# The fold of a unit in two steps, with another unit's masks in between, and one pair of logits behind a key copy

## The chip, the cores and the metric

The kernel runs on one core of one Trainium2 chip. The metric is the device time of one execution in microseconds (us). Engines are named as the profile names them: PE (matrix multiply; PEld is its weight load), DVE (vector), ACT (scalar), POOL (GpSimd) and SP, which here only issues DMAs. A name with a q behind it is the engine's sequencer or queue.

## The reference

Two blocks, one after the other, for 4 batches, 8 heads, 768 tokens and 48 channels per head (384 channels in all), in float32.

```python
f = 1.0 / (1.0 + np.exp(-f_logit))                       # attention with a gate
for t in range(S):
    state = f[:, :, t, :, None] * state + np.einsum('bhd,bhe->bhde', k[:, :, t], v[:, :, t])
    y[:, :, t] = np.einsum('bhd,bhde->bhe', q[:, :, t], state)

X = np.fft.fft(np.fft.fft(x, axis=1), axis=2)            # x: y as (B, S, H*D)
u = x + np.real(X)
un = (u - mean(u)) / np.sqrt(var(u) + 1e-06)
out = u + np.maximum(un @ w_ch1, 0.0) @ w_ch2            # 384 -> 1536 -> 384
```

## The kernel before

**Units.** Two heads of one batch make a unit: 16 units, unit u belongs to batch u // 4. Each unit is a Python generator, `attention(u)`, that goes on in `outputs(u)`; each `yield` ends a step. The steps, with their lines before the change: (1) the logits, two activations on ACT (L330, L331); (2) a running sum on DVE (L337, L338; L339 on POOL); (3) exponentials on ACT (L342, L343, L345); (4) two products on DVE (L349, L350); (5) 48 score matmuls (L361) into two PSUM tiles `sc`; (6) the masks: two copies under a mask on DVE, one per `sc` tile (L368); (7) the keys transposed on PE (L506, tile `st`) and copied by ACT to `kT` (L508); (8) `ds` on PE (L517); (9) a scan of the states on DVE (L525); (10) and (11) `y` on PE (L537, L544) and its copies on ACT (L553 to L557, tile `yT`); (12) transposes back (L564) and a copy to `x` (L566); (13) the fold.

`sc`, `st`, `ds` and `yt` share two PSUM buffers in turn, so the transposes of step 7 have to wait for the first mask of step 6, and `ds` for the second.

**The fold** adds and subtracts the halves of a batch's tokens, so that the Fourier transform over tokens needs less work. Its first part (L590 to L596) makes `eo` from `x`; L590 and L594 to L596 are on POOL, or on DVE in the last unit of a batch, and L591 to L593 on DVE. In the first two units of a batch it ends there. In the third and fourth a second part follows on DVE: `xs` (L604) and `xc` (L608), which read `eo` also in what POOL wrote, and in the fourth also `se` (L606), a second `xs` (L607), and `ce` and `xc` (L610 to L612).

**The Fourier part**, `fnet(b)`, begins with four terms `z` on PE (L650): from `se`, `xs`, `ce` and `xc` in this order, each against the table `tab`. ACT copies each term to `zz` (L653 to L657). The terms, and much else, use a PSUM pool of two buffers (`ps_f`): the third term needs what the copies of the first release. Then come `mid` (L684) and `mix` (L669) on PE, the sum with `x` and the moments on DVE (L686, L687, L725, L691, L692, L728, L730), a normalised row `un` (L705), its transposes `pt` (L708), and the two layers `up` (L750) and `fx`, `fz`, `po` (L773, L759).

**Tables and weights.** `tables()` (word T) issues the loads of `tab` and, from POOL, one indirect DMA (L183). `sort_tables()` (word S) puts them in order on POOL: L197 and L198 on `tab`, then L201 to L209 on `cd` and `half`, which `mid` and `mix` read. The weights come as 64-bit words; `weights()` (word C) turns a block into float32 with ACT (L238), DVE (L240, L241) and POOL (L242).

**What sets the order.** The order is written out by hand: `ORDER` is a string of words, and each word makes one piece of the program issue its instructions. A number runs the next step of that unit; `D` issues four matmuls without use (L153) that keep PE busy; `L7fk` issues the DMAs of unit 7's f and k; `F0`, `H0` and `P0` run steps of batch 0's Fourier part and layers; `r` fetches weights. Every engine executes its own instructions in the order in which the words issued them, and waits for the others by semaphores alone.

Of the kernel before, what the change touches and what calls it, by code (L numbers as in the profile page):

```python
# [12 lines left out]
C = 128  # L13
# [14 lines left out]
    "Gq2 r I D Gq0 L0f Gk1 L1f D Gk0 L0q i D Gq3 C Gq1 Z L0k 0 D 1 Gk2 0 L1q 1 L1k D D D D D D D D D D D "  # L28
    "D 0 0 1 0 r 1 L2f 0 2 C L1v 1 L3fk 1 3 L0v 0 1 L2q 2 0 0 r 1 L2k 3 1 0 2 r 3 L3q 2 L2v 0 C L3v C "
    "L4fk R 4 2 2 3 1 0 C 2 4 1 3 L5qv D L4qv L5fk 3 D D 3 2 0 2 3 2 3 C r 4 1 4 L6fk C r 2 5 4 L6qv 4 2 "  # L30
    "1 5 6 3 4 D 4 C 5 3 T 3 6 4 5 5 4 2 r L7fk 7 5 D L7qv 3 5 S L8fk C 4 7 6 6 5 F0 5 r r F0 F0 F0 7 4 "
    "C F0 L9fk 5 6 8 H0 H0 6 5 6 r H0 C L8qv 6 7 L9qv P0 6 7 r C P0 7 7 C 9 P0 r r 5 8 C r C F0 r 7 F0 6 "
    "P0 5 9 C 6 7 P0 r C P0 8 8 C P0 r r 7 P0 P0 8 9 H0 C P0 P0 8 7 8 C P0 H0 7 9 6 H0 H0 C 9 r C P0 9 "
    "L10fk r 9 P0 r C 9 L11fk 10 C 6 P0 11 4 P0 P0 P0 P0 P0 P0 10 P0 P0 P0 L10qv P0 P0 7 F1 9 P0 F1 H0 9 "
    "W P0 P0 P0 11 F1 P0 L11qv P0 P0 P0 9 P0 P0 P0 8 L12fk P0 11 11 8 P0 P0 10 11 F1 P0 11 11 10 L14fk "
    "F1 8 P0 14 F1 P0 10 P0 8 10 P0 P0 H1 H1 10 L12qv P0 P0 10 P0 F1 P0 11 11 10 P0 10 H1 P0 P0 P0 P0 12 "
    "12 12 P0 P0 12 P0 H1 P0 12 P0 H1 L13fk P1 P1 P1 P1 P1 14 13 P1 12 8 8 P1 P1 12 9 10 L13qv 13 P1 P1 "
    "L14qv 9 P1 12 11 P1 H1 11 10 P1 P1 13 P1 13 P1 12 P1 P1 14 P1 14 V 13 P1 c V 10 P1 P1 P1 P1 P1 V "
    "L15fk P1 13 P1 11 V P1 P1 P1 P1 c P1 11 F2 V c F2 F2 H1 13 H1 F2 c 14 P1 c V c P1 P1 12 P1 P1 14 P1 "
    "P1 13 V V V P1 15 F2 c P1 12 P1 P1 P1 P1 c P1 H2 14 15 V V P1 P1 P1 P1 P1 13 P1 14 F2 P1 c P1 P1 15 "  # L40
    "V 13 P1 H2 P1 P1 L15qv P1 14 13 P1 V 12 H2 F2 14 P2 P2 P2 P2 P2 P2 P2 15 P2 P2 P2 c c 12 H2 V H2 15 "
    "H2 15 P2 c P2 15 P2 P2 15 P2 14 13 15 P2 P2 14 P2 P2 15 13 P2 P2 P2 P2 P2 H2 V 15 P2 P2 14 15 H2 P2 "
    "P2 P2 P2 15 F3 F3 P2 F3 F3 P2 F3 c P2 P2 P2 P2 P2 V P2 c P2 V c c V P2 P2 P2 P2 P2 c P2 F3 F3 P2 V "
    "P2 H3 P2 P2 P2 H3 H3 P2 P2 P2 P2 P2 P2 P2 P2 P2 P2 P3 H3 c P3 P3 P3 P3 V P3 c P3 P3 P3 c V V c P3 "
    "P3 P3 H3 P3 P3 P3 P3 P3 P3 c P3 P3 V P3 H3 P3 P3 P3 P3 P3 P3 H3 H3 P3 P3 P3 P3 P3 P3 P3 P3 P3 P3 P3 "
    "P3 V P3 P3 P3 P3 P3 c P3 c P3 P3 P3 M P3 P3 P3 P3 P3 P3 P3 P3 P3 P3 P3 P3"
)

PAIRS = ((0, 3), (2, 5), (1, 4))
# [4 lines left out]
def kernel(  # L54
# [14 lines left out]
    B, HP, _, D, _, S = qkf.shape  # L69
# [426 lines left out]
    def outputs(u, x_all, AT, Q, K, te, T=None):  # L496

        hp = u % HP
        vt = v_of.pop(u)
        ps = ps_a.tile([128, 2, 512], F32, tag="sc", name=f"st{u}").rearrange("p a b -> p (a b)")
        for c in range(NCH - 1):
            nc.tensor.transpose(ps[:, c * 128:c * 128 + R], K[:, c * C:(c + 1) * C], ident[:R, :R])  # L506
        kT = p2.tile([128, NCH - 1, R], F32, tag="kT", name=f"kT{u}")
        nc.scalar.copy(kT, ps[:, :(NCH - 1) * 128].rearrange("p (c k) -> p c k", k=128)[:, :, :R])  # L508
        yield

        ps = ps_a.tile([128, 2, 512], F32, tag="sc", name=f"ds{u}")
        ds = ps[:, 0, :NCH * D].rearrange("p (e c) -> p e c", c=NCH)
        for c in range(NCH - 1):
            for r in range(2):

                n = 1 if c < NCH - 2 else 2
                nc.tensor.matmul(ds[FILL[r], :, c:c + n], lhsT=kT[:, c, FILL[r]],  # L517
                                 rhs=vt[:, c, r * D:(r + 1) * D].unsqueeze(2).to_broadcast([128, D, n]),
                                 start=True, stop=True)
        yield  # L520

        st = p2.tile([128, D, NCH], F32, tag="st", name=f"stt{u}")
        if te is not None:
            flat = lambda a: a.rearrange("p e c -> p (e c)")
            nc.vector.tensor_tensor_scan(flat(st[:R]), ps[:R, 0, :NCH * D], flat(te), 0.0, ALU.add, ALU.mult)  # L525
        else:
            nc.vector.tensor_copy(st[:R, :, 0], ds[:R, :, 0])
            for c in range(1, NCH - 1):
                nc.vector.scalar_tensor_tensor(st[:R, :, c], st[:R, :, c - 1], T[:, c:c + 1], ds[:R, :, c],
                                               ALU.mult, ALU.add)  # L530
        yield

        y = y_out

        for c in range(NCH):
            for r in range(2):
                nc.tensor.matmul(y[FILL[r], c * C:(c + 1) * C],  # L537
                                 lhsT=vt[:, c, r * D:r * D + (64 if r == 0 else D)], rhs=AT[:, r, c],
                                 start=(c % 4 == 0), stop=(c == 0), skip_group_check=True)
        yield  # L540

        for c in range(1, NCH):
            for r in range(2):
                nc.tensor.matmul(y[ROWS[r], c * C:(c + 1) * C], lhsT=st[ROWS[r], :, c - 1],  # L544
                                 rhs=Q[ROWS[r], c * C:(c + 1) * C], start=False, stop=True,
                                 skip_group_check=True)


        yT = p2.tile([128, S], F32, tag="yT", name=f"yT{u}")[:R]
        to = yT.rearrange("p (a n) -> p a n", n=C)  # L550
        rest = yT[:, 4 * C:].rearrange("p (a n) -> p a n", n=C // 2)
        of = y[:R, :S].rearrange("p (a n) -> p a n", a=4)
        nc.scalar.copy(to[:, 0:4:3, 1:], of[:, 0::2, 1:C])  # L553
        nc.scalar.copy(to[:, 1:3, 1:], of[:, 1::2, QS - 1:QS - C:-1])
        nc.scalar.copy(rest[:, 0::3], of[:, 0::2, C:])
        nc.scalar.copy(rest[:, 1:3], of[:, 1::2, QS - C:0:-1])
        nc.scalar.copy(to[:, 0:4, 0], of[:, :, 0])  # L557
        if te is None:
            load(u + 4, "q", "v")
        yield  # L560

        ps = ps_a.tile([128, 2, 512], F32, tag="sc", name=f"yt{u}").rearrange("p a b -> p (a b)")
        for c, i in enumerate((0, 1, 4, 2, 3, 5)):
            nc.tensor.transpose(ps[:, c * 128:c * 128 + R], to[:, i], ident[:R, :R])  # L564
        x = x_all()
        nc.scalar.copy(  # L566
            x[:, :, hp * 2 * D:(hp + 1) * 2 * D].rearrange("t c (r e) -> t c r e", r=2),
            ps[:, :NCH * 128].rearrange("t (c r k) -> t c r k", r=2, k=64)[:, :, :, :D])
        yield
        fold(u, x)  # L570

    eo_of = {}

    def fold(u, x):

        b, hp = divmod(u, HP)
        if b not in eo_of:
            eo_of[b] = p1.tile([128, 8, DM], F32, tag="eo", name=f"eo{b}")
        eo = eo_of[b] if hp < HP - 1 else eo_of.pop(b)
        ch = slice(hp * 2 * D, (hp + 1) * 2 * D)
        f = eo[:, :, ch]
        last = hp == HP - 1
        other = nc.vector if last else nc.gpsimd
        other.tensor_tensor(f[:, 6:3:-1], x[:, 0:3, ch], x[:, 3:6, ch], ALU.subtract)  # L590
        nc.vector.tensor_tensor(f[:, 1:4], x[:, 0:3, ch], x[:, 3:6, ch], ALU.add)  # L591
        nc.vector.tensor_tensor(f[:, 0:8:7], f[:, 1:7:5], f[:, 2:6:3], ALU.add)
        nc.vector.tensor_tensor(f[:, 2:6:3], f[:, 1:7:5], f[:, 2:6:3], ALU.subtract)  # L593
        other.tensor_copy(f[:, 1:7:5], f[:, 0:8:7])  # L594
        other.tensor_copy(f[0:1, 0], f[0:1, 2])
        other.tensor_tensor(f[0:1, 2:7:4], x[0:1, 0:2, ch], x[0:1, 3:5, ch], ALU.subtract)  # L596
        if hp < HP // 2:
            return


        lo, hi = (QD + 1, HD) if hp == HP // 2 else (1, QD + 1)
        up = slice(DM - lo, DM - hi, -1)
        tt = nc.vector.tensor_tensor
        tt(xs[:, :, lo:hi], eo[:, 4:7, lo:hi], eo[:, 4:7, up], ALU.subtract)  # L604
        if last:
            tt(se[:, :, 1:QD], xs[:, :, 1:QD], xs[:, :, HD - 1:QD:-1], ALU.subtract)  # L606
            tt(xs[:, :, 1:QD + 1], xs[:, :, 1:QD + 1], xs[:, :, HD - 1:QD - 1:-1], ALU.add)  # L607
        tt(xc[:, :, lo:hi], eo[:, 0:4, lo:hi], eo[:, 0:4, up], ALU.add)  # L608
        if last:
            nc.vector.tensor_copy(xc[:, :, 0:HD + 1:HD], eo[:, 0:4, 0:HD + 1:HD])  # L610
            tt(ce, xc[:, :, 0:QD + 1], xc[:, :, HD:QD - 1:-1], ALU.add)
            tt(xc[:, :, 0:QD], xc[:, :, 0:QD], xc[:, :, HD:QD:-1], ALU.subtract)  # L612
# [270 lines left out]
    with tc.If(again > 0):  # L883
# [13 lines left out]
        for b in range(B):  # L897
            x = p2.tile([128, NCH, DM], F32, tag="x", name=f"again{b}")
# [76 lines left out]
```

## Time and profile before

| | |
|---|---|
| median of 4 runs | 553.88 us (553.18 to 555.04) |
| the profiled execution | 554.22 us, its span 552.4 us, mean PE clock 0.983 |
| busy share of the span | PE 95%, PEld 84%, DVE 54%, ACT 35%, POOL 17% |
| chain that ended last | PE 88%, DVE 3%, DMA 2%, POOL 2%, ACT 2% |
| largest lines of the chain | PE up L750 34%, fx L773 16%, fz L773 12%, z L650 4% |

The span is what the profiler saw on the core; the device time has 1.8 us more around it. A line of the timeline gives the start and the length in us, the engine, the source line, the operation, the tile that is written and the tiles that are read, and in brackets how long the engine stood idle before it and who ended that. The releaser in the bracket is inferred: it is the last of the candidates to have ended. A line of the windows gives the length and then for PE, PEld, DVE, ACT and POOL the busy time with the number of instructions, and at the end the PE clock that was granted (1.00 is full), the share of DMA time, and GB/s.

### The profile page before, as it was taken

The page shows a single profiled execution, that of the slowest core. Times are in us where ns is not written, and L with a number is a line of the kernel's source. Part 1 is how long each engine was busy: PE and PEld are TensorE (multiplying, and loading weights), DVE is VectorE, ACT ScalarE, POOL GpSimd, SP SyncE. Part 2 cuts the span into 40 slices and gives each one's busy share as a digit, 9 for nine tenths or more (in the row PEclk, how much of TensorE's full clock was granted, in tenths as well). Part 3 has the DMA queues.
Part 4 walks back from the last instruction along what each step waited for, and adds up shares of the span by engine and source line. Part 5 has one row for each costly group of instructions (what it writes and reads, how often), then busy time and mean ns, then how long its engine had stood idle before and what let it go on. Part 6 is the DMA issues. An engine that isn't in the chain of part 4 may idle for free.

```text
span 552.4 us, 10204 instructions
## 1 busy us (share of the span) xinstructions
PE 526.7 (95%) x4186; PEld 462.0 (84%) x4186; DVE 300.0 (54%) x534; ACT 192.4 (35%) x497; POOL 94.9 (17%) x147
## 2 busy tenths in 40 slices
PE   6787699999999999999999999999999999999995
PEld 5676578876898889889889899899889798989985
DVE  8999899984936427436644344444452441413231
ACT  6767466671332432441340422321411303021110
POOL 6155635534001000120101001003001000010000
PEclk9798889999999999999999999999999999999999
DMA  8989636363202100412530401002002004000001
GB/s 229 272 222 230 180 115 162 123 187 95 67 0 72 42 3 2 116 44 65 178 115 15 115 1 59 28 1 87 1 28 87 1 13 159 0 30 0 30 2 34
DMA packets 18398, 44.38 MB, mean 80 GB/s; under 512 B 3109, under 2 KB 4710, under 8 KB 18342
## 3 DMA queue, kind: packets, MB, share of 16 engines
q1 hardware_dynamic: 17094, 39.89, 25.7%
q0 software_dynamic: 1104, 3.54, 1.8%
q8 instruction: 35, 0.57, 0.4%
q10 hardware_dynamic: 144, 0.20, 0.1%
q14 instruction: 21, 0.17, 0.1%
HBM read 38.90 MB, written 4.72 MB: 79 GB/s over the span
## 4 chain that ended last, share of the span: by engine, by line
PE 88%; DVE 3%; DMA 2%; POOL 2%; ACT 2%; issue 1%; ACTq 0%; POOLq 0%; DVEq 0%
PE up L750 34%; PE fx L773 16%; PE fz L773 12%; PE z L650 4%; PE y L537 3%; PE sc L361 3%; PE y L544 3%; PE po L759 3%; PE mix L669 3%; PE ds L517 2%; PE yt L564 2%; DMA tab<-in_seq_tab_dram,back 1%; PE pt L708 1%; PE st L506 1%; DVE at L368 1%
## 5 line engine op out<-in xcount | busy, mean ns | idle before, releaser
L750 PE MATMUL up<-unT,w 128*128 128x256 f32 x864 | 197.0, 382 | 1.5 <-DVE x L728 0.9
L750 PEld LDWEIGHTS up<-unT,w 128*128 128x128 f32 x864 | 160.9, 190 | 26.1 <-issue 1.5
L752 ACT ACTIVATE h<-up 128x256 f32<-128x256 f32 x144 | 55.1, 382 | 199.6 <-PE up L750 199.6
L617 POOL DMA_INDIRECT out_dram<-x,place x16 | 16.9, 1056 | 270.4 <-DVE x L803 233.7
L773 PE MATMUL fx<-block,h 128*128 128x192 f32 x264 | 46.5, 326 | 0.0
L773 PE MATMUL fx<-w,h 128*128 128x192 f32 x264 | 44.9, 327 | 0.1
L773 PEld LDWEIGHTS fx<-w,h 128*128 128x128 f32 x264 | 43.1, 190 | 0.8 <-ACT h L752 0.4
L773 PEld LDWEIGHTS fx<-block,h 128*128 128x128 f32 x264 | 43.5, 190 | 0.0
L780 DVE TENSOR_TENSOR s<-h,h 128x768 f32<-128x768 f32 x11 | 10.5, 955 | 50.4 <-ACT h L752 50.4
L242 POOL TENSOR_TENSOR w<-w,raw 128x384 uint32<-128x384 uint32 x24 | 29.9, 1250 | 46.3 <-ACT raw L238 18.9
L361 PE MATMUL sc<-q,W 48*64 48x128 f32 x768 | 26.1, 281 | 6.5 <-issue 3.6
L368 DVE COPY_PREDICATED at<-causal,sc 128x768 f32<-128x768 uint32 x32 | 31.3, 1031 | 1.1 <-PE sc L361 1.1
L361 PEld LDWEIGHTS sc<-q,W 48*64 48x64 f32 x768 | 21.6, 136 | 10.2 <-issue 5.9
L337 DVE TENSOR_TENSOR_SCAN W<-g,bound 112x768 f32<-112x768 f32 x16 | 29.5, 1844 | 0.5 <-issue 0.4
L725 DVE TENSOR_TENSOR x<-mix,x 128x384 f32<-128x384 f32 x12 | 6.7, 556 | 38.9 <-PE mix L669 38.9
L537 PE MATMUL y<-at,v 128*64 128x128 f32 (+1 forms) x384 | 26.7, 291 | 0.0
L537 PEld LDWEIGHTS y<-at,v 128*64 128x64 f32 (+1 forms) x384 | 23.0, 139 | 3.2 <-issue 3.2
L773 PE MATMUL fz<-w,s 128*128 128x192 f32 x132 | 23.5, 328 | 0.0
L773 PE MATMUL fz<-block,h 128*128 128x192 f32 x132 | 23.5, 328 | 0.0
L773 PE MATMUL fz<-w,h 128*128 128x192 f32 x132 | 23.4, 327 | 0.0
L773 PEld LDWEIGHTS fz<-w,s 128*128 128x128 f32 x132 | 21.6, 190 | 0.3 <-issue 0.3
L773 PEld LDWEIGHTS fz<-block,h 128*128 128x128 f32 x132 | 21.6, 190 | 0.3
(145 smaller groups left out, 730.4 us busy)
## 6 DMA issues: line engine op xcount, KB each, us to landing
raw<-in_w_ch_dram SPq DMA_DIRECT2D x24, 384.0 KB, 4.5
g<-in_qkf_dram SPq DMA_DIRECT2D x32, 144.0 KB, 4.0
q<-in_qkf_dram SPq DMA_DIRECT2D x32, 144.0 KB, 4.0
k<-in_qkf_dram SPq DMA_DIRECT2D x32, 144.0 KB, 5.1
v<-in_v_dram SPq DMA_DIRECT2D x16, 288.0 KB, 4.9
k<-in_w_ch_dram SPq DMA_DIRECT2D x12, 384.0 KB, 3.8
g<-in_w_ch_dram SPq DMA_DIRECT2D x12, 384.0 KB, 4.2
out_dram<-x SPq DMA_DIRECT2D x4, 168.0 KB, 2.1
```

The costliest lines, as they stand in the source:

```text
L242: nc.gpsimd.tensor_tensor(bits, bits, lo, ALU.add)
L337: nc.vector.tensor_tensor_scan(W, g, bound[:R], 0.0, ALU.add, ALU.min)
L361: nc.tensor.matmul(ps[64 * s:64 * s + 64, r, i * C:(i + 1) * C], lhsT=W[ROWS[r], o + 64 * s:o + 64 * s + 64], rhs=Q[ROWS[r], o:o + C], sta ...
L368: nc.vector.copy_predicated(AT[:, :, half], causal.bitcast(U32).unsqueeze(1).unsqueeze(1).to_broadcast([128, 2, NCH // 2, C]), ps[:, :, :N ...
L537: nc.tensor.matmul(y[FILL[r], c * C:(c + 1) * C], lhsT=vt[:, c, r * D:r * D + (64 if r == 0 else D)], rhs=AT[:, r, c], start=(c % 4 == 0), ...
L544: nc.tensor.matmul(y[ROWS[r], c * C:(c + 1) * C], lhsT=st[ROWS[r], :, c - 1], rhs=Q[ROWS[r], c * C:(c + 1) * C], start=False, stop=True, s ...
L617: nc.gpsimd.indirect_dma_start(out=out.rearrange("b s d -> (b s) d"), out_offset=bass.IndirectOffsetOnAxis(ap=place[:, b, i:i + 1], axis=0 ...
L650: nc.tensor.matmul(z[:, cols], lhsT=src[:, j, lo:hi], rhs=tab[:, t, T % 2, cols], start=(i == 0), stop=(i == len(parts) - 1), skip_group_c ...
L669: nc.tensor.matmul(mix[:, o], lhsT=zz[:rows_of[T], T, PLACES[c]], rhs=cd[:rows_of[T], T, :NQ - odd], start=(i == 0), stop=(i == 1))
L750: nc.tensor.matmul(pp[:, :256], lhsT=w1[:, kt, m * 128:(m + 1) * 128], rhs=unT[:, kt], start=(kt == 0), stop=(kt == 2))
L752: nc.scalar.activation(hs[-1][:, m % H].rearrange("p t n -> p (t n)"), pp[:, :256], AF.Relu)
L773: nc.tensor.matmul(out, lhsT=h[:, m], rhs=blocks[i][:, m], start=(start and m == 0), stop=(m == H - 1), skip_group_check=True)
```

## The change

`fold` becomes a generator that yields between its two parts, so the second part needs a word of its own in `ORDER`. Units 2, 3, 6, 7, 10, 11, 14 and 15 (those with a second part) have 14 words instead of 13. In seven of them the new word stands directly behind the old one. In unit 2 the masks of unit 5 (its sixth step) stand between. And unit 7's first step, which stood ahead of those masks, goes behind the seventh step of unit 5, the transposes and the copy of its keys.

```diff
         yield
-        fold(u, x)
+        yield from fold(u, x)
...
         if hp < HP // 2:
             return
+        yield
...
-    ... 5 5 4 2 r L7fk 7 5 D L7qv 3 5 S L8fk C 4 7 6 6 5 F0 ...
+    ... 5 5 4 2 r L7fk 5 2 D L7qv 3 3 5 7 S L8fk C 4 7 6 6 5 F0 ...
-    ... 10 C 6 P0 11 4 ...
+    ... 10 C 6 6 P0 11 4 ...
```

The last pair stands for the places of units 7, 10, 11, 14 and 15 too, where a second number stands behind the first in the same way. Behind `ORDER` the source lines move down by one, and behind the new `yield` by two: L330 becomes L331, and L604 becomes L606.

In the order of each engine this leaves two differences. DVE: from L593 (unit 2), L604 and L608 (unit 2), two L368 (unit 5), L590 (unit 3) to L593, two L368, L604 and L608, L590. ACT: from L566 (unit 3), L330 and L331 (unit 7), L508 (unit 5), L238 to L566, L508, L330 and L331, L238. The order on PE, POOL and SP is the same as before.

## The prediction

> **What bounds the kernel now.** I read the page first, then the windows, then the chain that ended last, and then the timeline of each engine around the edit. TensorE is busy for 95% of the span, so a change counts only where it lets TensorE start sooner. The windows say where that can be:
>
> ```profile
> 65.00:70.00 5.00, 2.77 (x23) 1.89 (x18) 4.72 (x12) 3.36 (x11) 3.80 (x10) 0.89 0.32 93
> 100.00:552.00 452.00, 444.00 (x3087) 394.11 (x3085) 207.66 (x393) 127.75 (x353) 47.90 (x67) 1.00 0.18 53
> ```
>
> The columns are PE, PEld, DVE, ACT, POOL busy, then the clock. After 100 us PE is packed at full clock, so a shift in its start there lasts to the end. Between 65 and 70 us PE works 2.77 of 5 us while DVE works 4.72: this stage is DVE's. The edit lies just ahead of it. On PE and DVE:
>
> ```profile
> 64.63 0.85 PE L517 MATMUL ds<-v,kT 128*64 128x48 f32 x20
> 67.70 1.70 PE L650 MATMUL z<-tab,se 128*95 128x385 f32 x6 [2.23 <-POOL half L207]
> 69.19 2.77 PE L650 MATMUL z<-tab,xs 128*96 128x385 f32 x6
> ...
> 58.98 0.36 DVE L593 TENSOR_TENSOR eo<-eo 128x192 f32<-128x192 f32 x1
> 60.83 0.46 DVE L604 TENSOR_TENSOR xs<-eo 128x285 f32<-128x285 f32 x1 [1.49 <-POOL eo L596]
> 61.66 1.96 DVE L368 COPY_PREDICATED at<-causal,sc 128x768 f32<-128x768 uint32 x2
> 63.52 0.43 DVE L590 TENSOR_TENSOR eo<-x 128x288 f32<-128x288 f32 x1
> 67.15 0.46 DVE L606 TENSOR_TENSOR se<-xs 128x285 f32<-128x285 f32 x1
> ```
>
> DVE stands 1.49 us at unit 2's second step (L604) until POOL has finished the first; unit 5's masks, whose scores are ready, queue behind it. PE stands 2.23 us before the first Fourier product.
>
> The bracket names POOL L207, and so does the chain. I do not believe it: z reads `tab` and `se`. POOL's last write of `tab` is L198, and L207 writes `half`, which z never reads. POOL and the sequencer of PE:
>
> ```profile
> 64.44 0.33 POOL L198 COPY tab<-pair 128x8 f32<-128x8 f32 x1
> 67.41 0.24 POOL L207 TENSOR_SCALAR_AFFINE_SELECT half<-half 128x1 f32<-128x1 f32 x1
> ...
> L650 PEldq EVENT_SEMAPHORE  x2: 51/1518/2986, 64.7 to 67.7; - x2
> ```
>
> `tab` is complete at 64.77. PE's sequencer sat on one semaphore for 2.99 us from 64.7. What ends at 67.61 is DVE's `se`; POOL's L207 ends at 67.65 by accident. So DVE gates z. ACT is the other queue that the edit touches:
>
> ```profile
> 62.03 0.84 ACT L330 ACTIVATE g<-g 112x768 f32<-112x768 f32 x1 [6.04 <-DMA g<-in_qkf_dram]
> 63.75 0.61 ACT L508 COPY kT<-st 128x560 f32<-128x560 f32 x1
> 67.41 0.48 ACT L345 ACTIVATE te<-deep,low 112x240 f32<-112x240 f32 x1
> 69.44 0.32 ACT L653 COPY zz<-z 95x192 f32<-95x192 f32 x1 [1.55 <-PE z L650]
> ```
>
> ACT runs without a break from 62.03 to 67.89 and then has 1.55 us to spare.
>
> The clock, in windows of 3.41 us:
>
> ```profile
> 65.48:68.90 3.42, 1.20 (x6) 0.90 (x7) 3.21 (x9) 2.32 (x6) 3.09 (x8) 1.00 0.35 121
> 68.90:72.31 3.41, 3.41 (x9) 2.24 (x8) 3.34 (x5) 0.90 (x5) 1.53 (x2) 0.50 0.00 0
> ```
>
> After 3.4 us with 1.2 us of PE work the granted clock is one half for the next 3.4 us. The same happens at 58.66 (1.25 us busy ahead of it) and at 45.00 (1.96 us ahead of it), but not at 55.24 (2.00 us). So about 2 us of work in such a window is the border.
>
> **The change, part by part.** The second step of the fold (L604 and, in a batch's last unit, L606 to L612) becomes a word of its own. For units 3, 6, 7, 10, 11, 14 and 15 that word stands right behind the first, so no instruction moves: nothing gained, nothing paid. PE's order, POOL's and SP's stay as they are everywhere, and no DMA is moved; the word D only issues PE work, and neither moved step issues any, so passing it costs nothing. Two things remain.
>
> *DVE.* Unit 5's two masks go ahead of unit 2's L604 and L608. They start when L593 ends, at 59.34, and not at 61.66; both score tiles are written by about 59.2 (PE L361, 57.48 + 1.76). Masks, xs and xc took 63.52 - 60.83 = 2.69 us, so unit 3's L590 starts at 59.37 + 2.69 = 62.06 instead of 63.52: 1.46 us sooner. The wait for POOL L596 (60.79) now falls under the masks (to 61.33), with 0.5 us to spare; without that cover it costs what it did, 1.49. Could the masks slow POOL's small steps L594 to L596, which they now run beside? POOL's L590 at 36.28 ran beside masks and took 0.79 us, its median; L594 beside a scan took 1.68 instead of 0.35. The masks are like the first row: I take zero. By the other row L594 would end just after the masks, L596 at about 62.5, and L590 would start at 63.4: a gain of 0.1 is left. That is the lower end.
>
> *ACT.* Unit 5's key copy goes ahead of unit 7's two activations. The transposes that it copies need mask one, which is now long done; they follow the D matmuls at about 62.6 and end at 63.3. So ACT stands idle from 62.03 to 63.3, copies until 63.84, and everything behind it is 1.3 us later: unit 7's logits, raw8's conversion, unit 4's y copies and unit 6's exponentials, which end at about 69.2 instead of 67.89. Who waits? Unit 7's scan takes its logits at 69.3, when they are done (65.6); unit 6's multiply takes its exponential at 71.8 (done 67.9); unit 4's transposes come at 72. Only the zz copies matter: z of the third term needs the PSUM buffer that the first zz copies release.
>
> *PE and what follows.* se is ready at 67.61 - 1.46 = 66.15, so z starts at 66.2 instead of 67.70. The idle gap is 0.9 us and the window to 68.90 holds over 2.6 us of PE work, so the clock should stay whole. A z term takes 1.30 us at full clock (397.00 to 398.31), so two terms end at 68.8. ACT copies the first from 69.2 to 69.8; the third term then runs to 71.15 and the fourth to 72.45 (before, yt began at 74.67). With yt (0.6), the last zz copies and mid (0.5), mix runs from about 73.6 to 75.1 instead of 75.9 to 77.4: 2.3 us sooner. DVE cannot follow all of that. Its queue, full from 63.5 on, is 1.46 sooner, and it also loses the 0.34 us for which L725 waited for mix: L725 at 75.65 instead of 77.45, **1.8 us**. From there PE's first transpose waits for DVE (0.17 and 0.39 us already today), so PE too moves by 1.8. From 80 to 552 us its listed waits come to 2 us, so little takes it back; the stream of weights (DVE L240 stood 1.68 us for a DMA at 123.28) might take 0.3.
>
> The sum: 554.22 (span 552.4 and 1.82 around it) - 1.8 = 552.4. That execution lies 0.34 above the median of 553.88, so against the median 552.1; with 0.1 for small losses I say **552.2**. Bounds of the unknown: 0.1 if the masks stop POOL; if the clock halves at 68.90 all the same, mix ends at about 76.25 and the gain is 1.15; if DVE kept pace with PE it would be 2.3.
>
> The Trainium skill ("TensorE: Matmul & The Clock Gate", Part 1) has the clock drop only after at least one idle window of about 3.4 us. The trace speaks against it: a gap of 2.2 us was enough. By the page the shorter gap would bring nothing through the clock, and the sum would be 1.46, thus 552.8 where the trace's row gives 552.4. The skill's "SBUF — State Buffer" ("Who interferes with whom") says that a VectorE instruction with two SBUF inputs and a GpSimd instruction that reads SBUF block each other. If that held for the masks the change would lose most of its gain; the 0.79 us row says that it does not.
>
> **The rivals.** *POOL is the gate, as the chain says* (no change): z would start at 67.7 whatever DVE does, and the time stays near 553.9. For it: the chain's own name and 40 ns between L207's end and PE's start. Against it: z reads nothing that L207 writes. With it I count a gain that is given back to the weight stream or to DVE before 130 us. Together 0.22.
>
> *ACT becomes the gate* (slower): the idle 1.3 us moves into ACT, the zz copies come late, and PE's gap moves from before the first z to before the third. My sum has ACT free at 69.2. It decides when ACT is free only after about 71.2, 2 us later than I work out: then the third term begins after 71.8, the gap of 3 us halves the clock for the next 3.4 us (1.7 us lost), mix ends at about 78.7, 1.3 us later than today, and the time is about 555.2. For it: ACT has no break from the key copy on. Against it: the 2 us of margin. 0.12.
>
> **How the numbers follow.** 0.2% is 1.1 us, about what a measurement of this kernel can tell from no change: faster means under 552.8. The forecast (1.15 to 2.3 us gained; 551.6 to 552.7) has 0.66. The range, 551.2 to 554.0, takes in the forecast with the spread of the runs below it and the no-change case, and leaves out the slow one.
>
> **What would show it.** Right: no POOL wait ahead of xs, unit 3's L590 near 62.1, z near 66.2 without a 2 us gap, clock 1.00 from 69 to 72, zz copies starting when ACT is free (69.2), L725 near 75.7, and PE everywhere 1.8 us sooner after 84. Wrong: z still at 67.7 (POOL gates), POOL's L594 over 1 us (masks block it), the third z term after 71.8 (ACT gates), or a new PE wait between 84 and 130 that eats the shift.

## The result and the profile after

The changed kernel takes 552.96 us (median of 49 runs) against 554.32 us for the kernel before (78 runs): 1.36 us less by the medians, ratio 0.9979 with a 95% interval of 0.9972 to 0.9987. It is inside the forecast range and on the forecast side; the gain is smaller than the 1.8 us of the sum, and lies between the 1.15 and 2.3 us of the forecast. The prediction counted from a median of 553.88 us over 4 runs; against the 554.32 us of 78 runs its 552.2 us misses by 0.8 us, the gain of 1.8 us by 0.4. The profiled execution is one of the longer ones of its kernel: 554.60 us, span 552.8, no shorter than the 554.22 us of the one profiled before. It shows what works and what does not.

DVE and PE of the changed kernel, by their timelines (source lines are one or two higher than before):

```profile
59.08 0.36 DVE L594 TENSOR_TENSOR eo<-eo 128x192 f32<-128x192 f32 x1
59.36 1.94 DVE L369 COPY_PREDICATED at<-causal,sc 128x768 f32<-128x768 uint32 x2
61.20 0.43 DVE L606 TENSOR_TENSOR xs<-eo 128x285 f32<-128x285 f32 x1
62.02 0.44 DVE L591 TENSOR_TENSOR eo<-x 128x288 f32<-128x288 f32 x1
65.10 0.62 DVE L608 TENSOR_TENSOR se<-xs 128x285 f32<-128x285 f32 x1
...
77.86 0.56 DVE L727 TENSOR_TENSOR x<-mix,x 128x384 f32<-128x384 f32 x1 [0.83 <-PE mix L671]
```

```profile
65.81 1.51 PE L652 MATMUL z<-tab,se 128*95 128x385 f32 x6 [0.55 <-POOL cd L204]
67.16 1.46 PE L652 MATMUL z<-tab,xs 128*96 128x385 f32 x6
70.72 2.11 PE L652 MATMUL z<-tab,ce 128*97 128x385 f32 x8 [2.10 <-ACT zz L657]
72.63 2.62 PE L652 MATMUL z<-tab,xc 128*96 128x385 f32 x8
76.25 1.57 PE L671 MATMUL mix<-cd,zz 97*128 97x193 f32 x8
```

The wait for POOL ahead of xs is gone, unit 3's fold starts at 62.02, and z starts at 65.81, 1.9 us sooner than before, without the gap of 2.23 us. Then a gap of 2.10 us stands ahead of the third term, and mix begins at 76.25, where it was 75.83. ACT says why:

```profile
63.26 0.62 ACT L509 COPY kT<-st 128x560 f32<-128x560 f32 x1 [7.24 <-PE st L507]
64.86 0.84 ACT L331 ACTIVATE g<-g 112x768 f32<-112x768 f32 x1 [0.98 <-DMA g<-in_qkf_dram]
69.72 0.48 ACT L346 ACTIVATE te<-deep,low 112x240 f32<-112x240 f32 x1
70.10 0.30 ACT L655 COPY zz<-z 95x192 f32<-95x192 f32 x1
```

ACT waits for unit 7's f, is at work without a break until 70.1, and copies the first term only then, though it was ready at about 67.3. The clock follows; in windows of 3.41 us:

```profile
68.07:71.48 3.41, 1.31 (x7) 0.67 (x6) 3.34 (x5) 3.00 (x10) 3.17 (x5) 1.00 0.59 149
71.48:74.90 3.42, 3.42 (x15) 2.58 (x14) 3.42 (x5) 0.66 (x4) 1.71 (x2) 0.51 0.45 134
```

Behind the length, the first number is PE's busy time and the sixth (without counting the brackets) is the clock: 1.31 us of work in one window, half the clock in the next. So in this execution the gap moved from before the first term to before the third and took the half clock with it.

### The profile page after: what moved, and what is told of

It reads as the page before. It is cut to its first block, busy times and chain, and to the rows that moved or that the text cites. A ratio compares the mean times of both kernels' runs of the same rounds, so it can differ in the third digit from the quotient of the medians.

```text
span 552.8 us, 10204 instructions
## 1 busy us (share of the span) xinstructions
PE 525.4 (95%) x4186; PEld 461.3 (83%) x4186; DVE 300.2 (54%) x534; ACT 192.3 (35%) x497; POOL 96.6 (17%) x147
## 4 chain that ended last, share of the span: by engine, by line
PE 87%; DMA 5%; ACT 2%; DVE 2%; SPq 1%; POOL 1%; issue 1%; ACTq 0%; POOLq 0%
PE up L752 34%; PE fx L775 16%; PE fz L775 12%; PE z L652 4%; PE y L538 3%; PE y L545 3%; PE sc L362 3%; PE po L761 3%; PE mix L671 3%; DMA raw<-in_w_ch_dram 2%; DMA g<-in_qkf_dram 2%; PE ds L518 2%; PE yt L565 1%; PE pt L710 1%; PE st L507 1%; DMA tab<-in_seq_tab_dram 1%
## 5 line engine op out<-in xcount | busy, mean ns | idle before, releaser
L243 POOL TENSOR_TENSOR w<-w,raw 128x384 uint32<-128x384 uint32 x24 | 28.5, 1193 | 46.0 <-ACT raw L239 25.9
L538 PE MATMUL y<-at,v 128*64 128x128 f32 (+1 forms) x384 | 25.1, 280 | 0.0
L538 PEld LDWEIGHTS y<-at,v 128*64 128x64 f32 (+1 forms) x384 | 21.5, 133 | 3.1 <-issue 2.9
```

The costliest lines, as they stand in the source:

```text
L243: nc.gpsimd.tensor_tensor(bits, bits, lo, ALU.add)
L538: nc.tensor.matmul(y[FILL[r], c * C:(c + 1) * C], lhsT=vt[:, c, r * D:r * D + (64 if r == 0 else D)], rhs=AT[:, r, c], start=(c % 4 == 0), ...
```

## The experiments

Theory A: ACT has become the gate of the third term, and the clock follows the gap. Theory B: DVE alone sets the gain, and what is missing from 1.8 us is the spread of the kernel before. Every run left one profiled execution. The start of unit 6's scan on DVE (L337 before, 51.1 to 53.0 us) serves as a mark: what an execution won or lost ahead of it is not counted. The mark is rough, since that scan took 3.25 us in most executions and 1.76 to 2.15 in some, so that the next one (L525) began 2.5 to 3.4 us behind the mark. The end of the stage is the first x from mix (before L725). In all 14 profiled executions the whole time lies 476.1 to 477.2 us behind that x, so **nearly all that the executions differ in has happened by then.** Times in us; "f" is where ACT began unit 7's logits.

| execution | scan | f | z | gap before third term | x from mix | scan to x | whole time |
|---|---|---|---|---|---|---|---|
| before | 51.54 | 62.03 | 67.70 | none | 77.45 | 25.9 | 554.22 |
| before, second | 51.37 | 65.45 | 69.17 | none | 78.29 | 26.9 | 555.12 |
| changed | 51.66 | 64.86 | 65.81 | 2.10 | 77.86 | 26.2 | 554.60 |
| changed, second | 51.76 | 65.35 | 65.68 | 2.73 | 78.34 | 26.6 | 555.14 |
| changed, third | 51.26 | 64.77 | 66.03 | 1.79 | 76.13 | 24.9 | 552.83 |
| masks only | 52.24 | 61.65 | 68.03 | none | 77.25 | 25.0 | 553.38 |
| logits only | 52.95 | 67.20 | 68.97 | 1.29 | 78.56 | 25.6 | 555.29 |
| late exponentials | 52.23 | 66.59 | 68.01 | none | 77.12 | 24.9 | 553.40 |
| late exponentials, second | 52.17 | 63.82 | 65.89 | none | 76.08 | 23.9 | 552.98 |
| early f | 51.34 | 64.55 | 65.96 | 1.61 | 76.02 | 24.7 | 552.79 |
| masks, early f | 52.03 | 57.57 | 66.84 | none | 77.21 | 25.2 | 553.70 |
| late exponentials, early f | 51.12 | 64.17 | 65.59 | none | 75.97 | 24.9 | 553.12 |
| fill | 51.62 | 64.08 | 65.44 | 0.38 | 75.65 | 24.0 | 552.07 |
| before, with fill | 52.18 | 62.48 | 69.15 | none | 78.54 | 26.4 | 555.01 |

**The changed kernel again, twice.** Nothing is changed.

> The changed kernel once more, for a second profiled execution. Theory A (ACT has become the gate of the third Fourier term, and the clock follows the gap): z starts near 66 as in the first profile, the third term starts only when ACT's first zz copies end, between 69.8 (unit 7's f landed early) and 70.7 (landed late), and the clock halves behind that gap when it is over about 1.4 us. Theory B (DVE alone sets the gain, and what is missing from 1.8 us is only that many executions of the kernel before did not have the half clock at 69 us): the third term starts within 0.5 us of the second's end and DVE's L727 near 75.7. Both: about 553.0 against 554.3 for the kernel before.

> The changed kernel a third time, for another profiled execution and for the comparison within this call. Theory A: a gap ahead of the third term of 1.0 us (f landed before 63.8) to 2.7 us (f landed at 65.4), the half clock behind it only with the longer ones, and the time of the execution going with them: about 552 without the half clock, 554.5 to 555 with it. Theory B: the third term follows at once.

Ratios to the kernel before: 0.9987 (0.9969 to 1.0005) and 0.9978 (0.9965 to 0.9991). Both executions have the gap ahead of the third term, so B's "the third term follows at once" is out. In the second the wait for f was 1.69 us, the third term began at 71.22, and the clock was half from 71 to 74.5. In the third the gap fell across two windows:

```profile
66.29:69.70 3.41, 2.56 (x12) 1.63 (x10) 3.31 (x8) 3.32 (x10) 1.64 (x3) 1.00 0.67 189
69.70:73.12 3.42, 2.49 (x15) 1.85 (x16) 3.38 (x4) 2.03 (x12) 2.77 (x2) 1.00 0.22 25
```

Each holds 2.5 us of work, the clock stays whole, and this execution took 552.83: 1.8 and 2.3 us less than the other two (0.4 and 0.5 us of that lie ahead of the scan).

**Only the masks.** ACT's order as before:

```diff
-r L7fk 5 2 D L7qv 3 3 5 7 S
+r L7fk 7 5 2 D L7qv 3 3 5 S
```

> The split of unit 2's fold with unit 5's masks in between, but unit 7's logits stay where they were, ahead of unit 5's key copy on ACT. Theory A: ACT has no 1.3 us of idle time ahead of the key copy, so where unit 7's f lands by 62 us the zz copies start by about 68, the third term follows the second without a gap, and the gain is 1.5 to 1.8 us; where f lands late (64.8) the key copy and with it ds wait until 66.5, z starts at about 68 and the gain is gone. Over many executions it lies near the changed kernel, 552.8 to 553.8. Theory B: the place of the logits is of no account; same time as the changed kernel.

Ratio 0.9994 (0.9976 to 1.0011): no gain that can be told. A had expected it near the changed kernel, and on the same occasion that one took 553.93 against 554.00 here (medians), so these runs do not tell the masks alone from the whole change. The profiled execution had f early (61.65) and, as A said for that case, the third term directly behind the second. Its z is late for another reason: POOL's indirect DMA (L183, 57.36, 2.12 us) ran ahead of unit 2's L590, and DVE stood 2.07 us for that where it stood 0.84 in the first profile.

**Only the logits.**

```diff
-r L7fk 5 2 D L7qv 3 3 5 7 S
+2 r L7fk 5 D L7qv 3 3 5 7 S
```

> Only the other half: unit 7's logits behind unit 5's key copy, the fold of unit 2 whole and ahead of unit 5's masks as in the kernel before. DVE's order is as before, so both theories have z at about 67.7 and no gain from DVE: the time of the kernel before, 554.3, within 0.4. Theory A has ACT free for the zz copies at 69.2 to 70.1, so the third term is at most 0.3 us later than without the edit.

1.0005 (0.9986 to 1.0023), as both said: without the masks' move there is no gain that can be told. The third term waited 1.29 us for ACT here too.

**Late exponentials.** Unit 6's third and fourth steps behind the first two Fourier terms; PE's order stays:

```diff
-C 4 7 6 6 5 F0 5 r r F0 F0 F0 7 4
+C 4 7 5 F0 F0 6 6 5 r r F0 F0 7 4
```

> The changed kernel with unit 6's exponentials (its third step, three activations of 2.1 us together on ACT) and the two DVE products behind them placed after the first two Fourier terms instead of ahead of them, so that ACT copies both terms to zz before it turns to the exponentials. Nothing else moves, PE's order is the same. Theory A: the first zz copies start at 67 to 68 instead of 69.2 to 70.1, the third term starts at 67.8 to 68.7 instead of 69.8 to 70.7, the gap is under 1 us, the clock stays whole from 68 to 75, mix ends near 74, and DVE, no longer waiting for mid and mix, has its L727 near 75.5: 0.6 to 1.5 us less than the changed kernel, about 552.2. Theory B: DVE sets the pace anyway; no change against the changed kernel (553.0).

> The changed kernel with unit 6's exponentials behind the first two Fourier terms, a second time on another occasion, since it is the version that beat both. Theory A: 0.6 to 1.5 us under the changed kernel of the same call, ratio to the kernel before near 0.996; the third term without a gap in the profile. Theory B: the first result was chance, ratio near 0.998.

0.9963 (0.9946 to 0.9980) and, on the second occasion, 0.9964 (0.9951 to 0.9976); by medians 552.91 and 552.45 against 553.93 and 553.23 for the changed kernel on the same occasions. This is what A expects, and it has the lowest medians of all versions. On each occasion by itself its interval still overlaps that of the changed kernel; over both, the mean of its 24 runs is 552.64 and that of the changed kernel's 24 is 553.61. Its PE, in the first profile:

```profile
68.01 1.54 PE L651 MATMUL z<-tab,se 128*95 128x385 f32 x6
69.38 1.46 PE L651 MATMUL z<-tab,xs 128*96 128x385 f32 x6
70.68 1.48 PE L651 MATMUL z<-tab,ce 128*97 128x385 f32 x8
72.00 1.48 PE L651 MATMUL z<-tab,xc 128*96 128x385 f32 x8
```

Four terms without a gap, each at full clock, although ACT took unit 7's logits only at 66.59. In the second profile PE stood 2.56 us for se and ran the first two terms at half clock, and the third still followed at once. The 23.9 us from scan to x, the least in the table, owe 0.8 us to the scan itself, which took 1.76 us here instead of 3.25.

**Early f.** The loads of unit 7's f and k ahead of the tables:

```diff
-5 3 T 3 6 4 5 5 4 2 r L7fk 5 2 D
+5 3 L7fk T 3 6 4 5 5 4 2 r 5 2 D
```

> The changed kernel with the loads of unit 7's f and k issued ahead of the Fourier tables on SP instead of behind the tables and one weight block. It takes the wait for f (0.98 and 1.69 us in two executions of the changed kernel) off ACT, and leaves ACT's order alone. Theory A: ACT takes unit 7's logits right behind the key copy, at 63.5 to 64, the first zz copies start near 69.2 and the third term near 69.8, so PE's gap is about 1.0 us instead of 2.1 to 2.7 and the clock stays whole behind it: 0.5 to 1 us less than the changed kernel. The price to watch: the tables land about 1 us later, which has to stay ahead of z (66). Theory B: f's landing does not matter; no difference.

0.9984 (0.9969 to 0.9998), no better by the medians than the changed kernel on its own occasions. In the profile f is no longer waited for and the clock stays whole, but the gap is 1.61 us and not 1.0: the key copy came at 64.02 and not 63.3, because half a clock ran until 63. So f's landing is one part of ACT's lateness, ACT's own queue the other, which is why the late exponentials help and this does little.

Two combinations, early f with the logits ahead of the key copy, and early f with the late exponentials:

> Early loads of unit 7's f and k as in the run before, and unit 7's logits back ahead of unit 5's key copy, where ACT stood idle from 56 to 62 us. Theory A: the logits run at about 58 to 60 in ACT's idle time, the key copy starts as soon as the transposes end, everything behind it is 1.8 us earlier than in the changed kernel, the first zz copies follow z without ACT being late, and no gap is left ahead of the third term: 0.7 to 1.5 us less than the changed kernel, as fast as the variant with the late exponentials. Theory B: no difference to the changed kernel.

> Late exponentials of unit 6 and early loads of unit 7's f and k together. Theory A: the two edits remove the same gap, so together they bring hardly more than the late exponentials alone, whose gap is already below 0.2 us: 552.0 to 553.0. Theory B predicts nothing for either.

Both failed: 1.0011 (0.9990 to 1.0031) and 1.0007 (0.9987 to 1.0027), where A had expected the best times. The mechanism that A describes is gone in both profiles (four terms without a gap, mix at 73.29 and 72.51, sooner than anywhere else), but DVE does not follow (in the first of them it also stood 2.08 us for POOL's L590), and PE has to wait for it: 2.01 us in the first. In the second:

```profile
78.68 0.52 PE L709 MATMUL pt<-ident,un 128*128 128x128 f32 x3 [1.67 <-DVE un L706]
```

Behind that gap the clock is half from 79.5 to 82.9. So in these two executions the lead at mix is lost again. Why the versions are slower than the late exponentials alone is not settled: the second execution took 553.12, well under the 554.55 of its version's median, so it need not show what the others lost, and early f by itself, the same move of the loads, cost nothing that can be told (0.9984).

**Fill.** Three words D between the second and the third term:

```diff
-F0 5 r r F0 F0 F0 7 4
+F0 5 r r F0 D D D F0 F0 7 4
```

> The changed kernel with three words D (12 matmuls without use, about 1.9 us at full clock) on PE between the second and the third Fourier term, where PE waits for ACT; ACT and DVE are untouched. It separates the clock from the wait. Theory A: the third term still starts when ACT's zz copies end (69.8 to 71.2), but the window around the gap now holds over 2 us of work, the clock stays whole behind it, the last two terms take 2.6 to 2.8 us instead of 4.4, and mix is about 1.5 us earlier than in the changed kernel's profile: 0.5 to 1 us less than the changed kernel in the executions where the gap fell into one window. Theory B: no difference, or slower by what the matmuls take if they delay the third term.

0.9988 (0.9971 to 1.0005), the changed kernel's own size. The profile has what A said (third term at 69.94, full clock, x at 75.65, and the shortest execution of all, 552.07), yet f was early there (64.08), and over 12 runs no gain shows. B is not confirmed by it, but the clock's share is not shown either.

**The same fill in the kernel before**, in the gap ahead of the first term:

```diff
-6 6 5 F0 5 r r F0
+6 6 5 D D D F0 5 r r F0
```

> The kernel before with three words D (12 matmuls without use, 1.9 us) on PE between unit 5's ds and the first Fourier term, in the gap of 2.2 us that the change shortens. No wait is removed: se still comes at 67.6. If the half clock at 68.9 is a consequence of that gap, it goes, the four terms take 5.3 instead of 7.1 us, mix ends near 75.6, DVE no longer waits for it, and the kernel is 0.3 to 0.8 us faster where the gap fell into one window: of the change's gain that part is the clock's. If the half clock there has another cause, the time stays at 554.3.

1.0012 (0.9995 to 1.0030): no gain. In its profile the clock is whole from 62 us on, the four terms take 5.3 us, and x from mix still comes 26.4 us behind the scan, with no wait of DVE for mix; 1.2 us of that are a longer wait of DVE for POOL's L590 ahead of the masks (2.07 us instead of 0.84). With the ratio it says that, where f is early (62.48 here), the half clock at 69 us is not what sets the stage of the kernel before: DVE does. (Where ds comes late, as below, the 12 matmuls also stand in front of z, so a small gain in the other executions may be hidden.)

**The kernel before, once more.**

> The kernel before, for a second profiled execution. Both theories: z at about 67.7 from the same start of unit 6's scan (16 us behind it), and a half clock behind the gap of 2.2 us unless a window of 3.4 us ends in its middle; x from mix about 26 us behind the start of unit 6's scan with the half clock, about 25.5 without.

The expectation was wrong, and this is the run that explains most. ACT and PE:

```profile
65.45 0.84 ACT L330 ACTIVATE g<-g 112x768 f32<-112x768 f32 x1 [9.11 <-DMA g<-in_qkf_dram]
67.17 0.61 ACT L508 COPY kT<-st 128x560 f32<-128x560 f32 x1
```

```profile
67.83 1.41 PE L517 MATMUL ds<-v,kT 128*64 128x48 f32 x20 [3.30 <-ACT kT L508]
```

Unit 7's f landed 3.4 us later than in the first profile. The key copy stands behind the logits on ACT, so PE waits 3.30 us for the keys; z starts at 69.17, gated by ds and not by se (67.4). The changed kernel had f as late (64.86, 65.35) and its key copies at 63.26 and 63.03.

## Why the prediction was right, and where its steps were not

*DVE.* Right up to se. Masks at 59.36 (59.37 in the sum), xs without a wait, unit 3's fold at 62.02 (62.06). POOL's small copy beside the masks took 0.35 us (59.57), as it did in the kernel before (59.47): the masks do not hold POOL up. se came a little sooner than worked out (L608 at 65.10, against 65.69), since unit 3's small steps were quicker: 0.26, 0.20 and 0.35 us for L595 to L597 against 0.42, 0.24 and 0.53. They used to run in the middle of POOL's sorting and now run at its start; that this is the cause was not tried. The end of the stage was to be 75.65; measured are 77.86, 78.34 and 76.13, with DVE standing 0.8 us for mix each time.

*POOL is not the gate of z.* Shown. z started at 65.81, before POOL had made `half`:

```profile
68.56 0.53 POOL L208 TENSOR_SCALAR_AFFINE_SELECT half<-half 128x1 f32<-128x1 f32 x1
```

The bracket now names another POOL line (cd L204), in the second execution tab L199, and in one of the late exponentials DVE's se itself. What is constant is that z starts 0.09 to 0.11 us after se ends, wherever ds was done by then.

*ACT.* This is the step that failed. I had ACT free at 69.2, the third term at 69.85 and a gap of about 1.0 us; measured are 70.0 to 70.6, 70.63 to 71.22, and 1.79 to 2.73 us. I took "62.03" of one execution for the landing of f, where ACT took it between 61.65 and 65.45 in the executions in which it waited for it, and so priced a wait on a DMA near its luckiest case: 0.98 and 1.69 us of wait in the first two executions, which the sum had at nothing. In the third that wait was 0.23 us, and the larger part was the key copy, 63.92 instead of 63.3, behind PE at half clock until 62.9. The gain at mix that I had at 2.3 us was a loss of 0.4 in the first profile, and a gain of 1.3 in the third.

*The clock.* In the stage of the changed kernel the border of about 2 us held: windows with 1.31 us of work (first execution) and 0.75 (second) halved the next, 2.5 us did not. It is not a rule of busy time alone. With only the masks moved, 1.66 us left the clock whole (first two lines); earlier in the second execution of the changed kernel, 1.66 us halved it (last two):

```profile
65.92:69.33 3.41, 1.66 (x16) 1.18 (x12) 3.20 (x9) 2.64 (x7) 3.08 (x9) 1.00 0.53 136
69.33:72.74 3.41, 3.41 (x20) 2.45 (x19) 3.32 (x5) 1.73 (x10) 1.74 (x2) 1.00 0.00 0
...
43.85:47.26 3.41, 1.66 (x49) 1.48 (x50) 3.19 (x5) 2.46 (x8) 1.60 (x3) 1.00 1.04 233
47.26:50.67 3.41, 3.41 (x28) 3.13 (x29) 3.27 (x5) 2.20 (x4) 1.85 (x2) 0.50 1.04 235
```

The first window held 16 matmuls, most of its time in the first Fourier term, the other 49, nearly all of them score matmuls; whether that is what counts was not tried. The slow rival had the right mechanism and too late a condition: I let it decide from an ACT that is free at 71.2, but 70.1 was enough, because half the clock came behind a gap of 2.10 us that lay in one window, not of 3 us. The Trainium skill ("TensorE: Matmul & The Clock Gate", Part 1) says the half clock comes after at least one idle window of about 3.4 us; here it came behind windows with 1.20, 1.31 and up to 1.97 us of work.

*The logits.* I counted their move as a pure cost of 1.3 us on ACT. The second execution of the kernel before shows what it buys: where f is late, PE stood 3.30 us for the keys, and z came at 69.17 where se alone would have let it start at about 67.5. The sum left this out, and it left out ACT's lateness on the other side; the two errors work against each other. That the measured gain came out near the sum is therefore in part luck. How often f is late in either kernel the runs do not tell, so the shares of the two halves stay open; by the one-sided runs neither half alone shows a gain, and of the three profiled executions of the changed kernel only the third is shorter than those of the kernel before by as much as the medians say.

*After the stage.* Right: from x to the end the profiled executions of both kernels take the same 476.8 us within 0.1, and PE's packed order keeps a shift to the end.

## What to carry to other kernels

When one engine's wait goes, lay out the queue of the engine that the change makes later, with each DMA it waits for at its latest landing in several executions and not at the one in the profile; a reorder that looks like a cost may be a guard against a late transfer. Then take the next waiter out as well: here three activations put behind the copies of two terms brought another 1 us or so, 0.9964 of the time before. Whether a gap on PE costs clock depended here on the window in which it fell (1.79 us over two windows did not, 2.10 us in one did); filling such gaps brought no gain that could be told, so look first whether PE, and not another engine, sets the end of the stage.

## What the runs showed of the hardware

The windows of the clock keep their own time: in the first profile the half clock began at 45.00, 58.66 and 68.90, which are 4 and 3 times 3.41 us apart, and it lasted for whole windows. The same program meets them at other places in every execution: in the changed kernel the third term began at 70.72, 71.22 and 70.63, and a window ended at 71.55, 71.15 and, counted on from 62.90, 69.73. Executions also differ ahead of the stage: in the 11 whose program is the same up to unit 6's scan, that scan began between 51.26 and 52.95 us. Whether the windows make that spread was not tried.

The landing of one and the same load, with the same DMA program ahead of it, moved by 3.4 us between two executions of the kernel before (62.03 and 65.45). And an indirect DMA on POOL (L183) occupied POOL for 1.17 to 2.16 us from one execution to the next. In three executions it both began late (56.8 to 57.4 us, against 56.11 in the first profile) and took 2.00 to 2.16 us, and DVE then stood 2.07 us or more for the subtraction behind it (L590) instead of 0.84.
